# Efficient attention and RWKV channel mix on one core: a planner's order against a written order table, with another opening and another last store

## The chip, the core and the metric

The kernel runs on one core of one Trainium2 chip. The metric is the device time of one execution in microseconds (us). Engines: PE is the matrix engine (TensorE; PEld its weight loads), DVE VectorE, ACT ScalarE, POOL GpSimd, SP the engine that only issues transfers. PE, ACT, DVE and POOL each run their own instructions in the order in which the program lists them. Transfers issued on SP and ACT go to the hardware's queues, those issued on POOL to a software queue; the sixteen DMA engines serve all of them.

## The reference

```python
# q, k, v: (8, 8, 576, 64) = batch, heads, S, D
q_s = softmax of q over D; k_s = softmax of k over S
kv  = einsum('bhsd,bhse->bhde', k_s, v)
x   = einsum('bhsd,bhde->bhse', q_s, kv), heads joined: (8, 576, 512)
x_prev = x moved by one row (a row of zeros first)
xk = mu_k * x + (1 - mu_k) * x_prev
xr = mu_r * x + (1 - mu_r) * x_prev
k   = max(xk @ w_k, 0);  v = (k * k) @ w_v      # w_k 512 x 1024, w_v 1024 x 512
out = sigmoid(xr @ w_r) * v                       # w_r 512 x 512
```

## The kernel before

**Work.** Attention goes by items (b, g): batch b, and g = 0 or 1 for half of the heads. An item is named by its two digits, so `KV01` is the product of batch 0, half 1. The channel mix goes by units of 512 rows (256 in the last unit of each half of the batches), ten in all; unit 0 needs batch 0 alone.

**Steps of an item.** `load..q/k/v` (`load`, L248; halves `0` and `1` for batches 0 and 1), `expq` and `expk` (L383, ACT), `rsum`, `rrec`, `scale` (L398, L402, L407, DVE: the softmax of q), `T` (L417, PE: 18 transposes of the scaled q into PSUM), `KV` (L438, L441, PE: 72 products; those with a column of ones, L441, give the sum of exp(k) and lie in the PSUM bank in which `T` wrote), `qt` (L424 or L428, ACT: copies the transposed q out of that bank), `rz` and `kvn` (L451 or L455, L461, DVE: reciprocal of the sums, scaled kv). For batches 0 and 1 the mix with mu is folded into the weights: `wp` (L538, DVE, two multiplications for xk, m = 0, and two for xr, m = 1), `X` (L550, PE, 16 products, per m) and `x` (L560 or L563, one copy by ACT and one by DVE, to xk or xr). From batch 2 on, `X`, `T` and `KV` of two items make one PE block `B`, and the mix is done on DVE after it.

**Steps of a unit.** `k` (L687, PE, eight groups of four 128x512 matmuls, each followed by `relu` L672 on ACT and `sq` L676 on DVE), `r` (L719, PE; `th` L724 on ACT), `v` (L739, PE, two halves of four matmuls per tile of 128 rows), `o` (L745, DVE) and the store `st` (L757, two transfers for each tile). A last digit or `.2` tells halves: in unit 0, `k01.2` is the second half of group 1.

**mu.** `emit_mu` (L313) makes, on PE in f32 before anything else, a wide copy of mu (L315, `mu_wide`) and, with four pairs of small matmuls, its transpose (L318); ACT copies the first, DVE makes 1 - mu from it (L328, `emit_rest`).

**What sets the order.** `Plan.order` (L158) runs a list scheduler over all operations with an assumed duration for each, due times (`AHEAD`, `SOON`, `LOOK`) and the free buffers; the program is written in the order of its start times. `FIRST` sets the queues of batch 0: of its eight half loads of q and k, seven go on SP and one, of item 01, on ACT. `gate` holds w_k's first load, and with it all that follows on POOL, until the ACT load has landed (`weight`, L341). The tile framework adds the waits between instructions from the tiles that they touch, and gives every transfer on POOL one of eight semaphores, so that a transfer waits until the one eight places earlier has landed.

Of the kernel before, what the change touches and what calls it, by code (L numbers as in the profile page):

```python
# [8 lines left out]
ACT = mybir.ActivationFunctionType  # L9
# [24 lines left out]
START = 0.7  # L34
HOP = 0.05
LATE = 1e6
LOOK = {"PE": 0.03, "ACT": 0.2, "DVE": 0.1, "POOL": 0.03, "SP": 0.03}
MAIN = 5.676
PACE = 1.116
DMA_LEAD = 2.0  # L40
DMA_TAIL = 0.6
LOAD_RATE = 375.0
CAST_RATE = 375.0
GATE = 5
FUSED = (0, 1)
ROWS = 1.05
MU_EARLY = 3.0
BLOCK_LOOK = 0.4
EARLY_UNITS = 2
AHEAD = {(0, 0): 0, (0, 1): 0.64, (1, 0): 3.95, (1, 1): 5.45, (2, 0): 10.46, (2, 1): 5.14, (3,  # L50
        0): 9.42, (3, 1): 7.74, (4, 0): 0, (4, 1): 10.55, (5, 0): 2.05, (5, 1): 11.13, (6, 0):
        16.45, (6, 1): 16.13, (7, 0): 1.76, (7, 1): 3.64}
FIRST = ((0, 0, ("SP", "SP")), (0, 1, ("SP", "SP")), (1, 0, ("SP", "ACT")), (1, 1, ("SP",
        "SP")))
SOON = {(1, 0, 0): 4.53, (1, 0, 1): 4.87}
PASSES = 3


class Slot:

    def __init__(self, pool):
        self.pool = pool
        self.index = None
        self.rank = self.since = None
        self.last = []


class Op:

    def __init__(self, engine, occ, lat, key, emit, deps, takes, gives, size, rate, name):  # L70
        self.engine, self.occ, self.lat, self.key = engine, occ, lat, key
        self.emit, self.deps, self.takes = emit, list(deps), list(takes)
        self.size, self.rate, self.name = size, rate, name
        self.start = self.end = self.made = None
        self.early = 0.0
        self.main = False
        self.look = 0.0
        for slot in gives:
            slot.last.append(self)


class Plan:

    def __init__(self):
        self.pools = {name: [SHARED.get((name, i), [(name, i)]) for i in range(n)]
                      for name, n in POOLS.items()}
        self.ops = []

    def add(self, engine, occ, lat, key, emit, deps=(), takes=(), gives=(), size=0.0, rate=1.0,
            name=""):  # L90
        op = Op(engine, occ, lat, key, emit, [d for d in deps if d is not None], takes, gives,
                size, rate, name)
        self.ops.append(op)
        return op

    def places(self, op):
        t, got = 0.0, []
        for slot in op.takes:
            if slot.index is not None:
                t = max(t, slot.since)  # L100
                continue
            best = None
            if slot.rank is not None and slot.rank != self.next.get(slot.pool, 0):
                return None
            for i, parts in enumerate(self.pools[slot.pool]):
                if (slot.pool, i) in got:
                    continue
                free = 0.0
                for part in parts:
                    user = self.user.get(part)  # L110
                    if user is not None:
                        if not user.last or any(o.end is None for o in user.last):
                            free = None
                            break
                        free = max(free, max(o.end for o in user.last) + HOP)
                if free is not None and (best is None or free < best[0]):
                    best = (free, i)
            if best is None:
                return None
            t = max(t, best[0])  # L120
            got.append((slot.pool, best[1]))
        return t, got

    def warm(self, t):
        busy = 0.0
        for s, e in reversed(self.pe_busy):
            if e < t - 3.4:
                break
            busy += min(e, t) - max(s, t - 3.4)
        return busy > 2.0  # L130

    def set_due(self):
        for op in self.ops:
            op.due = op.key
        for op in reversed(self.sorted):
            if not op.size and not op.main:
                for o in self.after[op]:
                    op.due = min(op.due, o.due - op.lat - HOP)
                op.due -= op.early

    def prepare(self):
        self.after = {op: [] for op in self.ops}
        for op in self.ops:
            for d in op.deps:
                self.after[d].append(op)
        left = {op: len(op.deps) for op in self.ops}
        ready = [op for op in self.ops if not op.deps]
        self.sorted = []
        while ready:
            op = ready.pop()  # L150
            self.sorted.append(op)
            for o in self.after[op]:
                left[o] -= 1
                if not left[o]:
                    ready.append(o)
        assert len(self.sorted) == len(self.ops)

    def order(self):  # L158
        self.set_due()
        self.user = {}  # L160
        self.next = {}
        self.pe_busy = []
        dma_free = 0.0
        out = {"HW": [], "SW": []}
        free, able, done = {}, {}, []
        left = {}
        for op in self.ops:
            op.start = op.end = None
            for slot in op.takes:
                slot.index = None  # L170
            left[op] = len(op.deps)
            able.setdefault(op.engine, [])
            if not op.deps:
                able[op.engine].append(op)
        n = len(self.ops)
        while len(done) < n:
            chosen = None
            for engine, ops in able.items():
                now = free.get(engine, START)
                ready = None  # L180
                for op in ops:
                    t = now
                    for d in op.deps:
                        t = max(t, d.end + HOP)
                    if op.size:
                        ends = out["SW" if op.engine == "POOL" else "HW"]
                        if len(ends) >= 8:
                            t = max(t, ends[-8] + 0.3)
                    if op.takes:
                        found = self.places(op)  # L190
                        if found is None:
                            continue
                        t = max(t, found[0])
                    rank = (max(t - op.look, now + LOOK[engine]), op.due)
                    if ready is None or rank < ready[0]:
                        ready = (rank, t, op)
                if ready is not None and (chosen is None or ready[1] < chosen[1]):
                    chosen = ready
            assert chosen is not None, "no operation can start"
            _, t, op = chosen  # L200
            fresh = [slot for slot in op.takes if slot.index is None]
            for slot, (_, i) in zip(fresh, self.places(op)[1] if fresh else ()):
                slot.since = t
                slot.index = i
                if slot.rank is not None:
                    self.next[slot.pool] = slot.rank + 1
                for part in self.pools[slot.pool][slot.index]:
                    self.user[part] = slot
            occ, lat = op.occ, op.lat
            if op.engine == "PE" and not self.warm(t):  # L210
                occ, lat = 2 * occ, occ + lat
            op.start, op.end = t, t + lat
            if op.size and op.size < 20:
                op.end = t + lat + (2.0 if op.engine == "SP" else 8.0)
            elif op.size:
                dma_free = max(dma_free, t + DMA_LEAD) + op.size / op.rate
                op.end = dma_free + DMA_TAIL
            if op.size:
                out["SW" if op.engine == "POOL" else "HW"].append(op.end)
            if op.engine == "PE":  # L220
                self.pe_busy.append((t, t + occ))
            free[op.engine] = t + occ
            able[op.engine].remove(op)
            done.append(op)
            for o in self.after[op]:
                left[o] -= 1
                if not left[o]:
                    able.setdefault(o.engine, []).append(o)
        return sorted(done, key=lambda o: o.start)
# [681 lines left out]
```

## Time and profile before

| | |
|---|---|
| median of 3 runs | 205.75 us (205.47 to 206.05) |
| the profiled execution's own time | 205.87 us |
| its span, first to last instruction | 204.1 us |
| around the span (difference) | 1.8 us |
| PE busy | 187.9 us, 92% |
| DVE, ACT, POOL busy | 152.7, 146.8, 38.6 us |
| last matmul ends | 198.82 us |

How to read it: times in the views count from the first instruction of the span. A busy PE in the opening is not PE at full speed, since the length of a matmul's row there is about twice that of the same row later. POOL's busy time is mostly the issuing of transfers.

### The profile page before, as it was taken

The page shows a single profiled execution, that of the slowest core. Times are in us where ns is not written, and L with a number is a line of the kernel's source. Part 1 is how long each engine was busy: PE and PEld are TensorE (multiplying, and loading weights), DVE is VectorE, ACT ScalarE, POOL GpSimd, SP SyncE. Part 2 cuts the span into 40 slices and gives each one's busy share as a digit, 9 for nine tenths or more (in the row PEclk, how much of TensorE's full clock was granted, in tenths as well). Part 3 has the DMA queues.
Part 4 walks back from the last instruction along what each step waited for, and adds up shares of the span by engine and source line. Part 5 has one row for each costly group of instructions (what it writes and reads, how often), then busy time and mean ns, then how long its engine had stood idle before and what let it go on. Part 6 is the DMA issues. An engine that isn't in the chain of part 4 may idle for free.

```text
span 204.1 us, 4851 instructions
## 1 busy us (share of the span) xinstructions
PE 187.9 (92%) x1930; PEld 93.9 (46%) x1930; DVE 152.7 (75%) x348; ACT 146.8 (72%) x226; POOL 38.6 (19%) x61
## 2 busy tenths in 40 slices
PE   0659999979999999999999999999999999999990
PEld 0445444534454444444466444444444444444750
DVE  1865478999889989999999995999825459622620
ACT  4463689999999999999999488777624752642520
POOL 4912269433223312532000000000000000000000
PEclk9999999999999999999999999999999999999997
DMA  6999999999999994999742220422044012404303
GB/s 206 277 247 206 256 404 391 399 405 405 392 393 400 410 385 137 368 348 401 224 102 53 48 58 3 100 57 53 0 100 110 0 41 65 103 0 103 90 16 104
DMA packets 16431, 40.10 MB, mean 197 GB/s; under 512 B 2196, under 2 KB 5528, under 8 KB 16408
## 3 DMA queue, kind: packets, MB, share of 16 engines
q0 software_dynamic: 9328, 27.99, 41.6%
q1 hardware_dynamic: 6696, 11.25, 19.7%
q10 hardware_dynamic: 384, 0.56, 0.8%
q8 instruction: 15, 0.25, 0.5%
q14 instruction: 8, 0.07, 0.1%
HBM read 33.56 MB, written 9.44 MB: 211 GB/s over the span
## 4 chain that ended last, share of the span: by engine, by line
PE 78%; DMA 13%; DVE 3%; ACT 2%; POOL 1%; issue 0%; DVEq 0%; ACTq 0%
PE mm_b L739 9%; PE mm_c L739 9%; PE mm_d L739 7%; PE mm_b L687 7%; DMA wr<-in_moe_w_r_dram 7%; PE mm_c L687 7%; PE mm_d L687 7%; PE mm_a L687 7%; PE mm_a L719 6%; DMA raw_g<-in_v_dram 4%; PE mm_a L739 4%; PE mm_d L719 3%; PE mm_c L719 3%; PE mm_b L719 3%; DMA raw_b<-in_q_dram 2%; PE att_b L444 1%
## 5 line engine op out<-in xcount | busy, mean ns | idle before, releaser
L687 PEld LDWEIGHTS <-wk_a 128*128 128x128 bf16 x160 | 15.3, 99 | 17.0 <-issue 1.8
L687 PEld LDWEIGHTS <-wk_b 128*128 128x128 bf16 x160 | 15.5, 98 | 15.3 <-issue 0.2
L719 PEld LDWEIGHTS <-xr 128*128 128x128 bf16 x144 | 13.9, 98 | 16.8 <-ACT xr L563 0.9
L739 PEld LDWEIGHTS <-k_a 128*128 128x128 bf16 x144 | 13.8, 98 | 16.4
L739 PEld LDWEIGHTS <-k_b 128*128 128x128 bf16 x152 | 14.2, 98 | 14.7 <-issue 0.2
L719 PE MATMUL mm_a<-wr,xr 128*128 128x512 bf16 x56 | 14.4, 379 | 0.4 <-DMA raw_g<-in_v_dram 0.4
L724 ACT ACTIVATE th_a<-mm_a 128x512 f32<-128x512 f32 x14 | 8.4, 602 | 7.2 <-PE mm_a L719 7.1
L687 PE MATMUL mm_b<-xk,wk_a 128*128 128x512 bf16 (+1 forms) x44 | 11.2, 371 | 0.0
L687 PE MATMUL mm_c<-xk,wk_a 128*128 128x512 bf16 (+1 forms) x40 | 10.2, 371 | 0.0
L687 PE MATMUL mm_a<-xk,wk_a 128*128 128x512 bf16 (+1 forms) x40 | 9.8, 360 | 0.3 <-DVE xk L560 0.3
L687 PE MATMUL mm_c<-xk,wk_b 128*128 128x512 bf16 (+1 forms) x40 | 9.4, 358 | 0.0
L687 PE MATMUL mm_d<-xk,wk_b 128*128 128x512 bf16 (+1 forms) x40 | 9.4, 358 | 0.0
L687 PE MATMUL mm_a<-xk,wk_b 128*128 128x512 bf16 (+1 forms) x40 | 9.4, 358 | 0.0
L687 PE MATMUL mm_b<-xk,wk_b 128*128 128x512 bf16 (+1 forms) x40 | 9.4, 358 | 0.0
L687 PE MATMUL mm_d<-xk,wk_a 128*128 128x512 bf16 (+1 forms) x36 | 9.2, 368 | 0.0
L315 PE MATMUL mm_a<-mu_rows,pick 2*128 2x512 f32 x2 | 2.0, 1122 | 6.8 <-DMA mu_rows<-in_moe_mu_r_dram 6.8
L719 PE MATMUL mm_d<-wr,xr 128*128 128x512 bf16 x32 | 8.2, 379 | 0.0
L719 PE MATMUL mm_b<-wr,xr 128*128 128x512 bf16 x28 | 7.2, 379 | 0.0
L719 PE MATMUL mm_c<-wr,xr 128*128 128x512 bf16 x28 | 7.2, 379 | 0.0
L676 DVE TENSOR_TENSOR k_a<-rel_a 128x512 bf16<-128x512 bf16 (+1 forms) x13 | 5.1, 391 | 2.8 <-ACT rel_a L672 2.6
L672 ACT ACTIVATE rel_b<-mm_a 128x512 bf16<-128x512 f32 (+1 forms) x7 | 4.0, 571 | 4.1 <-PE mm_a L687 3.9
L676 DVE TENSOR_TENSOR k_a<-rel_c 128x512 bf16<-128x512 bf16 (+1 forms) x13 | 5.1, 392 | 2.4 <-ACT rel_c L672 2.3
(323 smaller groups left out, 487.7 us busy)
## 6 DMA issues: line engine op xcount, KB each, us to landing
out_dram<-ot_a SPq DMA_DIRECT2D x14, 128.0 KB, 2.4
out_dram<-ot_b SPq DMA_DIRECT2D x14, 128.0 KB, 2.4
out_dram<-ot_c SPq DMA_DIRECT2D x14, 128.0 KB, 3.2
out_dram<-ot_d SPq DMA_DIRECT2D x14, 128.0 KB, 2.7
raw_k<-in_v_dram POOLq DMA_DIRECT2D x3, 576.0 KB, 8.5
out_dram<-ot_e SPq DMA_DIRECT2D x13, 128.0 KB, 2.4
raw_j<-in_k_dram POOLq DMA_DIRECT2D x2, 576.0 KB, 10.7
raw_a<-in_q_dram POOLq DMA_DIRECT2D x2, 576.0 KB, 10.1
```

Source lines behind the costliest of these rows:

```text
L315: nc.tensor.matmul(kn.bank(wide_slot), lhsT=kn.pick[:].rearrange("p u c -> p (u c)"), rhs=kn.mu_rows[:].rearrange("p m c -> p (m c)"), sta ...
L444: kn.nc.tensor.matmul(to, lhsT=by, rhs=kn.vvs[vv.index][two[r], j, u, 0:65], **flags)
L672: kn.nc.scalar.activation(out=kn.rels[rel.index][:, 0:n], in_=kn.bank(kf)[:, 0:n], func=ACT.Relu, scale=HALF_ROOT)
L676: kn.nc.vector.tensor_tensor(out=kn.k2s[k2.index][:, fc, 0:n], in0=kn.rels[rel.index][:, 0:n], in1=kn.rels[rel.index][:, 0:n], op=ALU.mult)
L687: kn.nc.tensor.matmul(kn.bank(kf)[:, 0:n], lhsT=kn.wk[fc // 4][:, ct, (fc % 4) * 128:(fc % 4) * 128 + 128], rhs=kn.xs[0][:, ct, c0:c0 + n] ...
L719: kn.nc.tensor.matmul(kn.bank(rps), lhsT=kn.xs[1][:, ct, c:c + 128], rhs=kn.wr[:, ct, :], start=(ct == 0), stop=(ct == CT - 1))
L724: kn.nc.scalar.activation(out=kn.ths[th.index][:], in_=kn.bank(rps), func=ACT.Tanh, scale=0.5)
L739: kn.nc.tensor.matmul(kn.bank(vps)[:, 0:width], lhsT=kn.k2s[k2.index][:, ft, 128 * m:128 * m + 128], rhs=kn.wv[ft // 4][:, ft % 4, part], ...
```

## The change

The scheduler with its durations and due times is taken out. `ORDER` lists all operations in one sequence, with the buffers that each takes behind a colon and, for one load, the issuing engine ahead of an exclamation mark; each engine runs its own operations in that sequence. Besides the order itself:

- The gate on w_k's load is gone. Of batch 0's loads, the first half of q of item 00 goes on ACT, seven on SP. On POOL, `load00v` comes first, then half loads of batch 1 between `load01v`, `wk0` and, later, `wk1`, `wr`, `wv0`, `wv1`.
- Up to sixteen operations `fill` are defined, two matmuls of 256 columns on a tile of zeros (`still`); the table uses six (`fill`, `fill.2` to `fill.6`).
- `KV` of batch 0 is cut into `KV000`, `KV001` (one for each half load of k), each of 36 products.
- The wide copy of mu stays in the opening (`wide`, `widecopy`); 1 - mu is made on POOL (`rest`). The transposed mu is loaded by two POOL transfers (`muload`) and made by one transpose (`mu`, `mucopy`) in unit 1.
- `wp` for m = 1 moves from DVE to POOL.
- The two transfers of each store are operations of their own. In the last unit the second one of tile 0 goes on POOL; those of tile 1 are on SP and ACT.

```diff
-FIRST = ((0, 0, ("SP", "SP")), (0, 1, ("SP", "SP")), (1, 0, ("SP", "ACT")), (1, 1, ("SP",
-        "SP")))
-SOON = {(1, 0, 0): 4.53, (1, 0, 1): 4.87}
-PASSES = 3
+FILLS = 16
+FIRST = ((0, 0), (0, 1), (1, 0), (1, 1))
+
+ORDER = """
+ACT!load00q0:0 zero load00v load01q1:1 warm load01q0 load10k0:2 load00q1 load00k1:3 ident rows
+load01v load00k0 load10q1:4 load01k0:5 wk0 expq000:0 load11q1:6 load01k1 expq011:1 rsum000:0
+load10v0:7 expq010 load10q0 rsum010:1 expq001 consts rsum001 wide:0 rrec000 expk001:0 rrec010
+rrec001 scale000:0 scale001 fill:1 expk000 rsum011 T00:0 widecopy fill.2:2 scale010:1 KV000:1 rest
+fill.3:3 rrec011 expk010:1 scale011 fill.4:1 KV001 qt00:0 wk1 T01:3 rz00:0 kvn00:0 fill.5:0
+load10k1 expk011 KV010:1 edge00 late qt01:1 load11q0 KV011 wp000:0 fill.6:1 rz01:1 expq101:2
+X000:0.2 kvn01:1 edge01 wp010:1 wp011 x0000 x0001 X010:3.1 wr k01:1 x0100 x0101 load11v0:8 k02:0
+expq111:0 rsum101:2 k03:2 load11k0:9 k00:3 load10v1 X011:0.1 expq100 k03.2 muload x0111 cast100:0
+k02.2 rsum100 k00.2 expk100:2 k01.2 wp001 x0110 relu02:0 load11v1 sq02:0 k04:0 rrec100 rsum111:3
+expk101 load11k1 X001:1.0 relu01:1 wv0 relu03:2 k06:1 expq110 sq03 rrec101 x0010 sq01 k05:2 x0011
+relu00:0 rsum110 relu04:2 r02:3 relu05:1 wv1 scale100:2 cast110:1 r01:0 sq05 load20v0:10 rrec111
...
+sq95 st82.2 v910:0 v811 r90:1 o81:4 k97:2 st81 th90:1 v900:3 relu97:0 sq97 v910.2:1 v911
+v911.2 v901 o90:2 o91.2:3 st90.2 st90 o91 st91.4 st91 st91.2 st91.3
+"""
...
+    def ordered(self):
+        ops = {op.name: op for op in self.ops}
...
+        for token in ORDER.split():
+            name, _, places = token.partition(":")
+            name, _, held = name.partition("^")
+            engine, _, name = name.rpartition("!")
+            op = ops[name]
+            if engine:
+                op.engine = engine
...
+            yield op
...
-    gate = [first[GATE]]
-        if gated:
-            kn.tc.add_manual_dep(ld.ins, gate[0].made.ins.name, sync)
...
-        for i in range(4):
-            nc.tensor.matmul(
-                kn.bank(mu_slot)[:, 2 * i:2 * i + 2],
-                lhsT=kn.mu_rows[:].rearrange("p m c -> p (m c)")[:, 128 * i:128 * i + 128],
-                rhs=kn.pick[:, :, 0], start=True, stop=True)
+    def emit_mu():
+        kn.nc.tensor.transpose(out=kn.bank(mu_slot)[:, 0:8], in_=kn.mu_sb[:],
+                               identity=kn.identf[:])
...
+        kn.nc.gpsimd.tensor_scalar(out=kn.mu_wide[:, 1, :], in0=kn.mu_wide[:, 0, :],
+                                   scalar1=-1.0, scalar2=1.0, op0=ALU.mult, op1=ALU.add)
...
+        def fill(slot=slot):
+            for _ in range(2):
+                kn.nc.tensor.matmul(kn.bank(slot)[:, 0:256], lhsT=kn.ident[:],
+                                    rhs=kn.still[:], start=True, stop=True)
...
-            kvm = add("PE", 0.9, 1.0, step, lambda: kv(kvp), before_kv + [tr], [kvp], leave_kv,
-                      name=f"KV{tag}")
+            kvm = tr
+            for u in range(2):
+                kvm = add("PE", lambda u=u: kv(kvp, (u,)), [expk[u], castv[0], consts, kvm], [kvp], leave_kv if u else [], name=f"KV{tag}{u}")
...
-                    kn.nc.vector.tensor_tensor(
+                    (kn.nc.gpsimd if m else kn.nc.vector).tensor_tensor(
...
-                        q = kn.nc.scalar if len(parts) == 2 and i == 1 else kn.nc.sync
+                    if last and m >= tiles - 2:
+                        queue = ("SP", "ACT" if len(parts) == 2 else "POOL")[i]
```

In the table's last line `o90` is the 512-column gate of tile 0 of the last unit (its matmuls `v901` are the last of the program); `o91` and `o91.2` are the two 256-column halves of tile 1, whose matmuls `v911` and `v911.2` come just ahead of `v901`. Before, DVE's order at the end is tile 0, then tile 1's first half, then its second half, whose matmuls come last.

## The prediction

> **What bounds the kernel now.** I read the page first, then busy time by stretch, then the timeline of PE in the opening, the waits, and the timeline of the last six microseconds.
>
> ```profile
> PE 187.9 (92%) x1930; PEld 93.9 (46%) x1930; DVE 152.7 (75%) x348; ACT 146.8 (72%) x226; POOL 38.6 (19%) x61
> ...
> 10.00:17.57 7.57, 5.40 (x199) 4.63 (x199) 5.15 (x15) 5.27 (x10) 1.08 (x2) 1.00 1.21 238
> 17.57:21.16 3.59, 3.59 (x26) 1.27 (x22) 1.42 (x7) 0.18 (x1) 0.72 (x2) 1.00 1.22 203
> 21.16:30.00 8.84, 8.11 (x67) 3.73 (x64) 5.61 (x13) 6.82 (x14) 3.69 (x8) 1.00 1.12 336
> 40.00:60.00 20.00, 18.85 (x245) 8.99 (x244) 18.75 (x38) 19.97 (x28) 6.85 (x10) 1.00 1.03 399
> 60.00:190.00 130.00, 130.00 (x1188) 62.09 (x1187) 103.61 (x225) 96.17 (x144) 11.97 (x17) 1.00 0.47 148
> ```
>
> In the stretches (length, then busy PE, PEld, DVE, ACT, POOL) PE is busy for all of 60 to 190 us. So the end is the moment at which unit 0's first `k` starts (17.57), plus a fixed amount of PE work, plus PE's idle and half-speed time behind that moment, plus the tail. Idle time behind it is small: 0.34 us at 22.11 and 1.15 us near 43. Half-speed time shows in the rows:
>
> ```profile
> 17.57 1.03 PE L687 MATMUL mm_a<-xk,wk_a 128*128 128x512 bf16 x2
> 18.39 1.06 PE L687 MATMUL mm_b<-xk,wk_a 128*128 128x512 bf16 x2
> 21.16 0.61 PE L687 MATMUL mm_d<-xk,wk_a 128*128 128x512 bf16 x2
> 22.55 0.59 PE L687 MATMUL mm_b<-xk,wk_a 128*128 128x512 bf16 x2
> 22.98 0.59 PE L687 MATMUL mm_c<-xk,wk_a 128*128 128x512 bf16 x2
> ```
>
> Two matmuls take 0.82 us from start to start at 17.57 and 0.43 at 22.55; the granted-clock column reads 1.00 in both stretches, so it does not show this. From 17.57 to 21.16 PE did three such pairs (1.29 at full speed) and one `X` (0.6 with the change of tile shape) in 3.59 us: 1.7 us lost to half speed.
>
> **The opening, as changed.** "Two hardware queues" is not new: one half load was on ACT before too. From issue time and time to landing, the SP half loads of before landed, in the queue's order, at 4.4, 5.3, 6.1, 8.6, 10.3, 11.7, 13.2. POOL's queue runs beside them from about 5 us in both kernels, so the same places give about the same times. In the new order they hold q of 01, q of 01, q of 00, k of 00 (no longer behind mu: 7.7), mu, k of 00 (10.1), k of 01 (11.7), k of 01 (13.3). Ungating w_k puts more behind v on POOL but takes no more of a shared rate; its first transfer starts 0.7 us earlier. I charge nothing; if POOL takes a larger share the chain shifts by up to 0.7.
>
> Now PE's order. mu lands 0.7 behind the load ahead of it (6.11 to 6.82 before), so at 8.4. `wide` takes 1.84 (6.82 to 8.66): 10.2. `fill`, two matmuls of half the width of the 17.57 row, 0.43: 10.7. `T00` 0.6 (10.29 to 10.88): 11.3. `fill.2`: 11.7. `KV000`, half of 13.32 to 14.40: 12.3. `fill.3`, `fill.4`: 13.1. `KV001`: 13.7, result 13.9. The three waits that follow come from one order: `qt00` now stands behind `KV001`, which writes the same PSUM bank. Before it stood ahead, and the sums waited for it:
>
> ```profile
> PE att_a L441 <- ACT qt_a L424: 1.0, 1, 1.0
> PE att_b L438 <- ACT ek_a L383: 0.9, 1, 0.9
> PE att_a L550 <- ACT xk L560: 1.2, 1, 1.2
> ```
>
> `qt00` (1.12) ends at 15.1; queued behind it on ACT is the second exp of k of 01, though its data lies ready (13.3): 15.7. `rz00` and `kvn00` (0.16 and 0.29) end at 15.6; `KV010` overwrites the bank that `kvn00` read, so 15.6 to 16.2. `qt01`, two copies (0.53 and 0.64), to 17.5; `KV011` writes its sums into the banks just read, so 17.5 to 18.2 with its result. `rz01` 0.25, `kvn01` 0.29, `wp010` 0.49: 19.2. Meanwhile `fill.6` and `X000` (0.94 at half speed, 15.37 to 16.32) go from 18.1 to 19.5; `X010` follows to 20.4; copies of `X000` (0.64 on ACT, two of 0.45 on DVE) end by 20.3. So `k01` starts near 20.4, 2.8 later than before. In that time `X010` is done too, worth 0.6: net 2.2 behind.
>
> What comes back. Before, the first full-speed row came 3.3 to 3.6 us behind the first dense one (17.57). Now dense work starts with `fill.6` at 18.1, so full speed at about 21.6, 1.2 us into `k`: 0.6 lost where 1.7 was, gain 1.1. The second gain is the idle time. `X011` (before, X waited for copies, and 0.34 and 1.15 were lost) now has other groups of `k` around it, and batch 1's attention is drawn forward to the first unit. If nothing new waits, 1.5 us come back. PE's end: 198.82 + 2.2 - 1.1 - 1.5 = 198.4.
>
> **Work moved to POOL.** DVE loses 0.69 (`rest`) and eight `wp` of 0.285. No row shows these on POOL; its affine select on 128x128 takes 0.29, its longest issue 0.84. I take 0.45 for a `wp`, with those two as bounds. `wp011` starts at 19.0 and `X011` is due at 22.1 behind four half groups: covered up to 1.5 each. Behind `wp011` on POOL stands `wr`'s issue (20), then five half loads of batch 1, two mu transfers, `wp001`, `wv0`, `wv1`. The queue's earlier bytes run out near 21.5, so `wr` (2.6 us, the spacing of w_k, w_r, w_v landings before) lands at 25 to 26, while `r02` is due at 27.5; `wv0` lands near 32, `v010` is due near 33.5. Cover of 1.5 us, not more. `muload`'s second transfer waits for `wk1` (about 21), and `wp001` behind it is due at 25. The Trainium skill, "GPSIMD Engine Reference", section "4.1 Engine selection", speaks against this move: it gives two-input elementwise work on GpSimd as about twice as slow as on VectorE. By that an estimate is 0.57 for a `wp`; the sum would stay. The transposed mu leaves the opening (1.63 us, 8.66 to 10.29) and costs one small matmul and its load in unit 1, under 0.1 on PE; that gain is inside the chain above, where the fills take 1.7 of it back. `identf` and the memset of `still` add about 0.2 to DVE ahead of 7.7, where `T00` is not due before 10.7: nothing. `KV` in two halves issues the same 72 products; its price is the order above. Single stores and the new column of mu in `scale_x` cost nothing that a row shows.
>
> **The tail.**
>
> ```profile
> 198.22 0.60 PE L739 MATMUL mm_a<-wv_b,k_b 128*128 128x256 bf16 x4
> 198.86 0.42 DVE L745 SCALAR_TENSOR_TENSOR ot_a<-th_b,mm_a 128x256 f32<-128x256 f32 x1 [0.24 <-PE mm_a L739]
> 198.88 1.19 SPq L757 DMA_DIRECT2D out_dram<-ot_a  x2
> 198.97 1.58 ACTq L757 DMA_DIRECT2D out_dram<-ot_a  x2
> ```
>
> Before, one gate of 0.42 follows the last matmul, and the span ends 5.28 behind it. Now `v901` is last and DVE runs `o90`, `o91.2`, `o91` behind it: starts 0.61 and 0.34 apart, the last ends 1.40 behind PE instead of 0.46. `o91.2` and `o91` had their matmuls 0.9 and 1.3 earlier, but stand behind `o90`. The two pairs of stores follow as before, so 0.94 later: 6.2 behind PE. `o90`'s POOL store starts at 0.8; with `vb_a`'s first-transfer delay as the upper bound (7.5 to landing with its data, 3.9 to its first packet) it could end last by up to a microsecond; the other loads on POOL bound it at 4, hidden. I take hidden.
>
> **Sum.** 198.4 + 6.2 = 204.6 of span, and 1.8 around it: 206.4, against 205.87 of the profiled execution (the median is 205.75). About 0.6 us (0.3%) is what a measurement of this kernel can tell.
>
> **The rivals.**
> *The zeros do their work (faster).* PE is busy from 8.4 on, and if full speed comes by about 12, `fill.3` to `X010` shrink by 0.9 and nothing is lost in `k` (0.6): 204.9. For it: six fills are dense. Against it: before, PE was busy for 5 of the 7.5 us from 10 to 17.57 and stayed at half speed. It decides if the first `k` row reads 0.43 per pair and starts before 19.5.
> *Full speed comes a window later (slower).* If dense work from 18.1 misses the moment, `k` runs at half speed for 4 to 5 us: 1.4 to 1.9 more lost, 208.1. The Trainium skill, "TensorE: Matmul & The Clock Gate", section "What's actually happening", says that the clock is judged over free-running windows of about 3.4 us, so a start inside one waits for the next. The 3.3 us of before agree with one whole window; the trace cannot show where it began.
> *A wait takes the place of the removed ones (slower).* `r02`, `v010` or `X011` wait on POOL's queue, or the 1.5 us of idle time reappear: 207.5 to 208.
> *The table does nothing that PE can feel* (dense part and opening cancel, tail overlapped): 205.5 to 206.2.
>
> **How the numbers follow.** Forecast, 206.0 to 206.9, 0.42, a third of it inside the bound. Zeros effective, 204.4 to 205.3, 0.23. Later window, 0.13. New wait or late POOL store, 0.12. Cancelling, 0.10. Faster: 0.23 and a little of the last: 0.25. Slower: 0.28 + 0.13 + 0.12 = 0.53. Same: 0.22. The range takes in the rivals on both sides, without the outer half of those that end late.
>
> **What would show it.** Right: `wide` near 8.4, `qt00` near 14, `k01` near 20.4, PE end near 198.4, DVE's last gate 1.4 behind it. Wrong: `k01` before 19, PE idle again between 22 and 45, a POOL row of `wp` over 1.5 us, or an end less than 5.6 behind PE.

## The result, and the profile after

The changed kernel takes 212.33 us (median of 4 runs, 211.38 to 212.61) against 205.68 for the kernel of before on the same chip: a ratio of 1.031, 95% interval 1.028 to 1.035. It is slower, as forecast, but by 6.7 us where 0.7 were forecast, and outside the range: the slowest rival on record stood at 208.1. The profiled execution of the changed kernel took 212.61, of it 210.8 of span.

From the page, the engines' busy time; then busy time by stretch (length, then busy PE, PEld, DVE, ACT, POOL; granted clock, DMA share, GB/s) for the opening, the first 6 us of `k`, and the two stretches behind:

```profile
PE 191.3 (91%) x1935; PEld 94.6 (45%) x1935; DVE 150.7 (71%) x341; ACT 146.6 (70%) x225; POOL 44.4 (21%) x73
```
```profile
10.00:24.21 14.21, 12.58 (x227) 7.68 (x226) 5.62 (x24) 6.54 (x11) 4.32 (x8) 1.00 0.94 251
24.21:30.00 5.79, 5.79 (x36) 2.38 (x36) 3.59 (x7) 4.52 (x9) 4.69 (x10) 1.00 0.92 219
30.00:60.00 30.00, 29.86 (x409) 14.34 (x408) 25.91 (x55) 28.49 (x44) 16.76 (x25) 1.00 1.02 329
60.00:190.00 130.00, 129.20 (x1190) 62.33 (x1189) 106.40 (x232) 98.79 (x149) 12.28 (x17) 1.00 0.50 164
```

The first `k` starts at 24.21 (17.57 before), although PE is busy for 12.6 of the 14.2 us ahead of it: the opening is for the most part not waiting, it is working. Behind it PE is idle for 0.14 near 41 and 0.80 between 60 and 190, where before it was never idle in the latter. The opening on PE's timeline:

```profile
9.65 2.04 PE L252 MATMUL mm_a<-mu_rows,pick 2*128 2x512 f32 x2 [9.65 <-DMA mu_rows<-in_moe_mu_r_dram]
11.62 0.61 PE L284 MATMUL mm_b<-still,ident 128*128 128x256 bf16 x2
12.16 0.66 PE L358 MATMUL att_a<-ident,qs_a 64*128 64x64 bf16 x18
...
13.29 0.27 PE L379 MATMUL att_b<-vb_a,ek_a 64*64 64x64 bf16 x2
...
14.22 0.20 PE L382 MATMUL att_a<-one,ek_a 64*64 64x1 bf16 x2
14.35 0.61 PE L284 MATMUL mm_d<-still,ident 128*128 128x256 bf16 x2
14.75 0.63 PE L284 MATMUL mm_b<-still,ident 128*128 128x256 bf16 x2
15.31 0.27 PE L379 MATMUL att_b<-vb_a,ek_a 64*64 64x64 bf16 x2
...
24.21 1.01 PE L589 MATMUL mm_b<-xk,wk_a 128*128 128x512 bf16 x2
25.02 1.06 PE L589 MATMUL mm_a<-xk,wk_a 128*128 128x512 bf16 x2
```

`wide` is 1.25 later than forecast. One half of the first sums step, 36 products, runs from 13.29 to 14.35: 1.06 us, as long as 68 of the 72 products took before (13.32 to 14.40; the other four had run earlier). The `k` pairs still start 0.8 apart: half speed. Further back, a late store on the chain of waits, and the rows of PE and VectorE where PE's 0.80 of idle time arises:

```profile
64.29 8.09 DMA out_dram<-ot_b
```
```profile
72.03 1.02 PE L589 MATMUL mm_a<-xk,wk_a 128*128 128x512 bf16 x4 [0.64 <-DVE ot_e L646]
73.21 1.02 PE L589 MATMUL mm_c<-xk,wk_b 128*128 128x512 bf16 x4 [0.16 <-DVE ot_b L646]
```

```profile
71.29 0.69 DVE L646 SCALAR_TENSOR_TENSOR ot_e<-th_a,mm_a 128x512 f32<-128x512 f32 x1 [1.34 <-DMA out_dram<-ot_e]
72.47 0.69 DVE L646 SCALAR_TENSOR_TENSOR ot_b<-th_b,mm_c 128x512 f32<-128x512 f32 x1 [0.49 <-DMA out_dram<-ot_b]
```

These are two waits, not one. The larger, 0.64, is the gate `o13` (71.29): the table gives it the buffer `ot_e`, which `o11` had used (62.42). That tile's two stores were issued right behind their gate, at 63.13 and 63.65, and the second landed at 71.17 in the trace's records, 7.5 us after its issue. The smaller, 0.16, is `o12` (72.47), which takes `ot_b`. The other half of that tile was stored at 44.54; this half, `st00.2`, stands behind `st03` and `st11` in SP's order, is issued 20 us later and lands at 72.38. The end:

```profile
202.53 1.03 PE L640 MATMUL mm_d<-wv_b,k_b 128*128 128x512 bf16 x4
203.59 0.69 DVE L646 SCALAR_TENSOR_TENSOR ot_c<-th_b,mm_d 128x512 f32<-128x512 f32 x1 [2.28 <-PE mm_d L640]
...
204.53 0.41 DVE L646 SCALAR_TENSOR_TENSOR ot_d<-th_a,mm_a 128x256 f32<-128x256 f32 x1
204.58 0.57 POOL L656 DMA_DIRECT2D out_dram<-ot_c  x1 [98.62 <-DVE ot_c L646]
...
204.97 1.14 SPq L656 DMA_DIRECT2D out_dram<-ot_d  x2
```

The last gate ends 1.38 behind PE (203.56), as forecast, and the last store lands at 208.32. But the span ends at 210.83, 2.5 behind that landing, where before it was 1.2 (202.86, 204.07). In the trace's records SP's closing drain ends at 208.77, and POOL's, which begins with its store at 204.55, ends at 210.05, though that store landed at 207.63.

### The profile page after: what moved, and what is told of

Its sections match the earlier page's. It is cut to its first block, busy times and chain, and to the rows that moved or that the text cites. A ratio compares the mean times of both kernels' runs of the same rounds, so it can differ in the third digit from the quotient of the medians.

```text
span 210.8 us, 4855 instructions
## 1 busy us (share of the span) xinstructions
PE 191.3 (91%) x1935; PEld 94.6 (45%) x1935; DVE 150.7 (71%) x341; ACT 146.6 (70%) x225; POOL 44.4 (21%) x73
## 4 chain that ended last, share of the span: by engine, by line
issue 48%; PE 31%; DMA 7%; DVE 6%; ACT 2%; SPq 1%; POOL 1%; POOLq 0%; DVEq 0%
PE mm_c L589 4%; DMA out_dram<-ot_b 4%; PE mm_a L589 3%; DMA mu_rows<-in_moe_mu_r_dram 3%; PE mm_d L589 3%; PE mm_b L589 3%; PE mm_a L640 2%; PE att_b L379 2%; PE mm_d L620 1%; PE mm_b L640 1%; PE mm_d L640 1%; PE att_a L473 1%; PE att_b L473 1%; PE mm_a L252 1%; PE mm_b L620 1%
## 5 line engine op out<-in xcount | busy, mean ns | idle before, releaser
L589 PE MATMUL mm_b<-xk,wk_b 128*128 128x512 bf16 (+1 forms) x56 | 13.1, 357 | 0.0
L589 PE MATMUL mm_d<-xk,wk_a 128*128 128x512 bf16 (+1 forms) x48 | 11.8, 361 | 0.0
L620 PE MATMUL mm_d<-wr,xr 128*128 128x512 bf16 x44 | 11.3, 380 | 0.0
L589 PE MATMUL mm_a<-xk,wk_a 128*128 128x512 bf16 (+1 forms) x40 | 10.6, 381 | 0.6 <-DVE ot_e L646 0.6
L620 PE MATMUL mm_b<-wr,xr 128*128 128x512 bf16 x40 | 10.3, 379 | 0.0
L589 PE MATMUL mm_d<-xk,wk_b 128*128 128x512 bf16 x36 | 9.2, 379 | 0.0
L589 PE MATMUL mm_b<-xk,wk_a 128*128 128x512 bf16 (+1 forms) x32 | 7.7, 354 | 0.1
L640 PE MATMUL mm_a<-wv_a,k_a 128*128 128x512 bf16 x28 | 7.2, 380 | 0.0
L640 PE MATMUL mm_a<-wv_b,k_a 128*128 128x512 bf16 x28 | 7.2, 379 | 0.0
L620 PE MATMUL mm_a<-wr,xr 128*128 128x512 bf16 x28 | 7.2, 379 | 0.0
L589 PE MATMUL mm_c<-xk,wk_b 128*128 128x512 bf16 (+1 forms) x32 | 6.9, 339 | 0.2 <-DVE ot_b L646 0.2
```

The source lines that it names most:

```text
L589: kn.nc.tensor.matmul(kn.bank(kf)[:, 0:n], lhsT=kn.wk[fc // 4][:, ct, (fc % 4) * 128:(fc % 4) * 128 + 128], rhs=kn.xs[0][:, ct, c0:c0 + n] ...
L620: kn.nc.tensor.matmul(kn.bank(rps), lhsT=kn.xs[1][:, ct, c:c + 128], rhs=kn.wr[:, ct, :], start=(ct == 0), stop=(ct == CT - 1))
L640: kn.nc.tensor.matmul(kn.bank(vps)[:, 0:width], lhsT=kn.k2s[k2.index][:, ft, 128 * m:128 * m + 128], rhs=kn.wv[ft // 4][:, ft % 4, part], ...
```

## The experiments

The theory after this reading: four separate costs, namely the sums in two steps, the fills, the late half store (to which it put down all of the 0.80), and the store on POOL, beside loads that land later. The rivals, for each, stand in the expectations. Times are medians, with the ratio to before from the same chip; "T00 to k" is the time from `T00`'s start to the first `k`, which leaves most of the effect of the loads out (12.05 in the changed kernel).

**e1, sums in one step.**
```
-            for u in range(2):
-                kvm = add("PE", lambda u=u: kv(kvp, (u,)), [expk[u], ...
+            kvm = add("PE", lambda: kv(kvp), expk + [castv[0], consts, kvm], ...
```


> The changed kernel with each b0 sums step (72 products) in one piece again, at the place of the second half. Theory A (a half of 36 products takes PE as long as the whole did, 1.06 us, so the two-step form costs 2.1 us on the opening chain): the second piece still takes 1.06 and the first is gone; unit 0's first k goes from 24.21 to about 22.1, and the time from 212.3 to about 210.2. Rival (a half costs half, and the late opening is the loads alone): the merged piece takes 2.1, first k stays within 0.3 of 24.2 and the time within 0.4 of 212.3.


209.54, 1.019 (1.015 to 1.023). T00 to k 9.58: 2.5 less; the loads were 0.9 earlier as well. PE's timeline of e1:

```profile
12.72 0.63 PE L282 MATMUL mm_b<-still,ident 128*128 128x256 bf16 x2
13.29 0.28 PE L377 MATMUL att_b<-vb_a,ek_a 64*64 64x64 bf16 x4
...
14.13 0.18 PE L380 MATMUL att_a<-one,ek_a 64*64 64x1 bf16 x4
...
14.61 0.39 PE L282 MATMUL mm_a<-still,ident 128*128 128x256 bf16 x2
...
18.16 0.61 PE L282 MATMUL mm_b<-still,ident 128*128 128x256 bf16 x2
...
38.01 1.02 PE L637 MATMUL mm_a<-wv_b,k_a 128*128 128x512 bf16 x4 [0.83 <-DMA wv_b<-in_moe_w_v_dram]
```

Four products stand in a row where the halves had two, and the last of all 72 starts 0.84 behind the first, the last rows already at full speed (see the last section). Theory A holds in kind. The 2.5 has a little of that full speed in it; e2 and e8 below, two kernels without fills that show none in the opening, are 1.7 apart with and without halves (e8 has edits to stores and POOL's queue besides). The last row of the view: with the opening shorter, `w_v` is too late, the wait that the prediction had named as a rival and that the late opening had hidden.

**e2, no fills** (the `fill` tokens taken out of the table).


> The changed kernel without its six groups of zero matmuls. Theory A (the zeros stand on the chain and bring no clock): the opening loses fill.2, fill.3, fill.4 from its chain (0.55 + 1.0), first k near 22.7, the same 0.8 us lost to half speed in k: 210.8. Rival (the zeros bring the clock forward): first k near 22.7, but half speed lasts 1.5 us longer into k, so the time stays at 212.3 within 0.4.


210.70, 1.025 (1.019 to 1.031). T00 to k 10.02, 2.0 less. Full speed came 2.5 to 4.0 us into `k` (1.9 in the changed kernel). Theory A by the time and for the chain. The profiled execution took 212.18, the slowest of four (209.39 to 212.18), and in it half speed lasts 2.0 longer into `k`, as the rival has it. Kernels that keep the fills show full speed anywhere from 0.4 to 3.8 behind the first `k` too, so this one profile does not decide for the rival.

**e3, stores at their gates.** In the table `st00.2` and the others follow their gates, and `o13:4 ... o12:1` becomes `o13:1 ... o12:4`.


> The changed kernel with SP's stores in the order of their gates, the two halves of a tile side by side (and output buffers 1 and 4 exchanged for o13 and o12, so that the one with the earlier store is used first). Theory A (PE's 0.8 us of idle time at 71 to 73 comes from one late half store, issued 20 us after its gate): no idle PE row between 60 and 200, PE's end 0.8 to 1.0 earlier, 211.4. Rival (the stores land late because the loads hold the DMA engines, wherever they are issued): 0.5 us or more of idle time stays at 70 to 75, and the time is within 0.4 of 212.3.


212.18, 1.031 (1.027 to 1.034). The 0.80 of idle time became 0.25, 0.4 more was lost to half speed in `k`, and PE's end came 0.5 earlier in the profile; in the times there is no difference: inconclusive alone. The edit has two parts. The exchange of the buffers bears on the 0.64: `o13` now takes a buffer that is free (70.30 instead of 71.29). The stores of `o11` still take 7.4 and 7.9 us to land, as the rival says, and `o12`, which now takes their buffer, is the 0.25 that is left. e8, with the same edit, has no such idle time; e1, e2, e4, e7, e13 and e14, without it, have 0.7 to 0.9 before the same gate.

**e4, the late store off POOL.**
```
-                        queue = ("SP", "ACT" if len(parts) == 2 else "POOL")[i]
+                        queue = ("SP", "ACT")[i]
```


> The changed kernel with the one late store that GpSimd issues (half of the tile o90) issued by ScalarE instead. Theory A (GpSimd's closing drain ends 2.4 us behind its own store's landing and 1.3 behind SP's drain, and so sets the end): the span ends 6.0 behind PE instead of 7.2, time 211.1. Rival (the three gates and pairs of stores behind the last matmul set the end, GpSimd's drain is covered): the end stays 7.0 or more behind PE, time within 0.3 of 212.3.


210.56, 1.024 (1.019 to 1.029). The end is 5.70 behind PE instead of 7.27. Theory A. (PE's end was 0.5 earlier as well, with full speed 0.4 behind the first `k`; the edit touches nothing there.)

**e5, the kernel of before with its sums in two passes.**
```
-            for j in range(J):
-                for u in range(2):
+            for u, j in ([(u, j) for u in range(2) for j in range(J)] if b == 0 else
+                         [(u, j) for j in range(J) for u in range(2)]):
```


> The kernel of before with one edit: in each of batch 0's two sums steps, all 36 products of the first half stand ahead of all 36 of the second, instead of alternating. Same instructions, same places for the step as a whole. Theory A (products of the two halves run beside each other on PE only when they alternate): each step takes 2.1 us instead of 1.08, first k from 17.57 to about 19.6, time 207.8. Rival (a product costs what it costs, 0.015 us, in any order): steps of 1.08, 205.7 within 0.3.


207.06, 1.0055 (1.003 to 1.008). The second step:

```profile
17.07 0.26 PE L439 MATMUL att_b<-vb_b,ek_b 64*64 64x64 bf16 x2
...
18.87 0.19 PE L442 MATMUL mm_d<-one,ek_b 64*64 64x1 bf16 x1
19.00 0.61 PE L688 MATMUL mm_a<-xk,wk_a 128*128 128x512 bf16 x1
```

From its first to its last start it takes 1.80, against 1.13 before (16.32 to 17.45), from nothing but the order of the same products. T00 to k is 7.96 instead of 7.28. Theory A in kind, 0.7 where it expected 2.0: the first step costs nothing, since its first half runs in the 0.89 that PE had waited for `k`'s exp. The other half of the 1.4 in time would be the loads, which were 0.75 later in this profile; why they were is not shown.

**e6, the kernel of before with two late stores on POOL** (`kn.nc.gpsimd` where `part.stop == C`). The expectation speaks of one; the edit also moves the second half of the last unit's next-to-last tile, whose part ends at C as well (198.90).


> The kernel of before with one edit: of the last tile's four half stores, the one that ScalarE issues last is issued by GpSimd. Theory A (a store on GpSimd's queue at the end holds GpSimd's closing drain 5.5 us from its issue, as in the changed kernel, 204.58 to 210.05): drain ends near 205.0, span near 205.7 instead of 204.1, time 207.3. Rival (GpSimd's store is as good as ScalarE's, and the longer tail of the changed kernel comes from three gates): 205.7 within 0.4.


207.62, 1.009 (1.006 to 1.013). From the timeline and from the chain:

```profile
199.88 0.55 POOL L757 DMA_DIRECT2D out_dram<-ot_a  x1 [0.43 <-DVE ot_a L745]
```
```profile
199.86 0.57 POOLq L906
```

POOL's drain runs from 199.86 to 205.16, 2.0 behind SP's (203.12). Theory A, shown a second time, though not for one store alone.

**e7, mu ahead of the first half load of k** (the token `rows` moved).


> The changed kernel with the mu rows loaded ahead of the first k half load, where before had them, instead of behind it. Theory A (the fifth half load falls into the pause of 5.5 to 7 us that GpSimd's first packets cause in SP's queue, and mu stands behind it): wide starts near 7.3 instead of 9.6, T00 near 10.2 instead of 12.2, first k 1.3 to 1.7 earlier, time 210.8. Rival (the chain runs through k's loads, which the mu rows push back): first k within 0.4 of 24.2, time within 0.4 of 212.3.


211.48, 1.029 (1.025 to 1.032). `wide` 7.59, `T00` 10.14, first `k` 22.24; T00 to k 12.10, unchanged. Theory A for the opening, 2.0 earlier; but 1.17 of idle time appeared at 93, again a gate that waits for a store (the buffer's store lands at 93.05, the gate starts at 93.13), and of the 2.0 only 0.85 is left.

**e8, the four together,** with `wr` ahead of `wp011` and `muload` behind `load20q0` on POOL.


> The changed kernel with the edits of e1, e2, e3 and e4 together, and on GpSimd's queue w_r ahead of the opening's wp, and the late mu transfers behind batch 2's first loads. Theory A (the four causes are separate and add up): first k near 18.7, no idle time over 0.3 behind it, full speed within 1.5 us of it, PE's end near 198, the end 5.7 behind it: span 203.7, time 205.4, even with before. Rival (w_v's loads are late once the opening is faster, as the 0.83 us wait at 37 in e1 shows): 1 to 2 us of idle time between 33 and 45, time 207.


205.35, 0.998 (0.996 to 1.0005). First `k` 19.55, idle time 0.14, PE's end 197.83, the end 5.69 behind it. Theory A: the costs add up (2.8, 1.6, 0.2 and 1.8 alone make 6.4, together 7.0), though the first `k` comes 0.85 later than it expected.

**e9 to e12, from e8 on.** e9: `v901 v910.2 ... v911 v911.2`, the gates and stores in that order. e10: `load10k0` behind `wk0`. e11: `nc.vector` for all `wp`. e12: `X000:0.2 KV011:1 ... k01:1 k02:0 X010:0.1`.


> e8 with PE's last products in another order: the full-width v901 ahead of the four half-width ones, so that a gate of 0.42 is last, as before. Theory A (one gate behind PE instead of three, as in before): the end 5.0 to 5.3 behind PE instead of 5.7, time 204.8. Rival (the landing of the stores, 3.4 behind the last gate, is set by how many are open at once, and they still come together): the end stays 5.6 or more behind PE, 205.3.


204.08, 0.992 (0.989 to 0.995). The end is 4.37 behind PE: Theory A, and more.


> e9 with the one half load of batch 1 that stands second on GpSimd's queue (2.3 KB packets, between the two v of batch 0) moved behind w_k's first half. Theory A (its packets take the DMA engines from SP's loads, which landed up to 1.2 later than before's): SP's last four half loads land 0.4 to 0.7 earlier, first k 0.4 earlier, time 204.4. Rival (SP's loads share packet by packet with whatever GpSimd sends): landings within 0.2, time within 0.3 of e9.


203.93, 0.991 (0.988 to 0.994), the same as e9. Three of SP's last half loads land 0.4 earlier than in e9 (8.8, 10.6 and 12.5), and the first `k` comes 0.4 earlier, as Theory A has it; but e11 and e12, with e9's loads, have 10.6 and 12.2 too. Not told apart.


> e9 with the four wp of m = 1 on VectorE again (the first of them behind the copies of X010). Theory A (wp010 on VectorE takes 0.75 instead of 0.45 because GpSimd's wp runs beside it, and this stands on the chain): the wp010 row 0.45, first k 0.3 earlier, time 204.5. Rival (VectorE needs the time that GpSimd took off it): first k as in e9, and 0.3 to 0.6 of idle PE time between 22 and 45, time 205.1.


202.91, 0.987 (0.984 to 0.990). `wp010` takes 0.49 (0.75 in e9), but T00 to k is 8.21 against 8.25: what it saves is hidden. PE's end is 1.13 earlier than in e9: 0.6 by the loads (`T00`), 0.13 of idle time, 0.1 of half speed; the rest was not found in rows.


> e9 with X000 ahead of the second sums step and X010 behind the first two groups of k, as before had it. Theory A (what counts is the total of PE's opening work and its half-speed time, not when k starts): first k near 17.8 instead of 19.5, but two more k groups at half speed and X010 to do; PE's end within 0.3 of e9, time 204.8. Rival (an earlier k is worth its whole lead): PE's end 1.0 or more earlier, time 203.6.


203.45, 0.990 (0.987 to 0.994). First `k` at 17.13, 2.7 earlier; PE's end 0.9 earlier: by these numbers and the time nearer to the rival. But `T00`, which the edit does not touch, is 0.6 earlier, and the 0.3 that is left is what Theory A has. Not told apart.

**e13 to e15.** e13: the changed kernel with `nc.vector` for all `wp`. e14: `memset(kn.still[:], 1.0)`. e15: e11 with e12's order.


> The changed kernel with one edit: the four wp of m = 1 on VectorE again, the first of them behind the copies of X010. Theory A (the move to GpSimd, priced at nothing, costs by itself: the loads of w_r and w_v and the copies behind wp on VectorE come later): first k 0.2 to 0.3 earlier, time 211.3 or less. Rival (the move is covered in the changed kernel, whose late opening leaves room): time within 0.4 of 212.3.


210.72, 1.025 (1.022 to 1.029). Faster by 1.6, as Theory A wants, but not by its mechanism: T00 to k is 12.04, `T00` itself 0.9 earlier (nothing ahead of it was touched), and full speed came 0.4 behind the first `k` instead of 1.9. What the move of `wp` costs by itself stays open; on the chain from `T00` to `k` it is nothing.


> The changed kernel with one edit: the fills multiply ones where they multiplied zeros. Theory A (it is not the zeros: the fills are too few and too spread to bring the clock, whatever they hold): the fills stay at 0.186 from one matmul to the next, full speed again only from 24.5 to 27, time within 0.4 of 212.3. Rival (zeros do not count as work for the clock, ones do): full speed before 17, the second sums step and X at half their time, first k near 21.5, time 209.


213.07, 1.034 (1.030 to 1.038). Fills 0.186 apart, full speed at 25.2: Theory A by these signs. The time is 0.7 over that of the changed kernel, outside the 0.4 that it allowed, with overlapping intervals; its profile has 1.27 of idle time at 95 before a gate, where the changed kernel, the same but for one constant, has none.


> e11 with the order of e12 in the opening (X000 ahead of the second sums step, X010 behind two groups of k). Theory A (PE's total counts, not the start of k): within 0.4 of e11, 202.7. Rival (the gains of e11 and e12 add up): 202.2 or less.


202.95, 0.987 (0.984 to 0.989): Theory A by the time. In the profile `T00` is 0.65 later than in e11 and PE's end 0.16 earlier, so what this order is worth stays open. e9 to e12 and e15 are all faster than the kernel of before, e11 and e15 by 1.3%. Of e11, the two stretches that had idle time in the changed kernel:

```profile
30.00:60.00 30.00, 30.00 (x454) 14.69 (x453) 26.45 (x58) 28.73 (x42) 12.98 (x18) 1.00 1.06 381
60.00:190.00 130.00, 130.00 (x1144) 63.02 (x1142) 103.04 (x225) 95.00 (x145) 10.84 (x15) 1.00 0.47 147
```

## Why the prediction was wrong in size

The direction held, and so did the frame: the first `k`, plus PE's work, plus what is lost, plus the tail. But the 0.7 of the forecast was hardly more than the 0.6 that it called measurable, the small rest of terms that cancelled, and most of the 6.7 comes from terms that it had too small or at nothing: that the sign came out right says little for the sum. By its terms, against the profiled execution:

| term | forecast | measured | more |
|---|---|---|---|
| `wide` starts | 8.4 | 9.65 | 1.25 |
| from there to the first `k` | 12.0 | 14.56 | 2.56 |
| lost to half speed in `k` | 0.6 | 0.9 | 0.3 |
| idle behind the first `k` | 0 | 0.94 | 0.94 |
| the end behind PE | 6.2 | 7.27 | 1.07 |
| time | 206.4 | 212.6 | 6.2 |

**The step that failed most: "`KV000`, half of 13.32 to 14.40", and "`KV` in two halves issues the same 72 products; its price is the order above".** A half takes as long as the whole. In the rows of before, four products share each 0.05 us, two for each half of the output partitions; in the changed kernel two do. The forecast counted products; it should have looked at which of them ran side by side. Four halves at 0.95 to 1.06 where 0.6 to 0.7 was taken are 1.5 of the 2.56; e1 (2.5 on T00 to k, with some full speed in it), e8 against e2 (1.7) and e5 (0.7 on one step) show it. Of the rest, 0.5 is the fills and 0.3 `X010` (22.98 to 24.21, where 0.9 was taken). The Trainium skill, "TensorEngine Tiling (Array Packing)", section "Key Properties", says that different tiles of the array work independently and in parallel; the traces agree: 1.1 us with the halves alternating, 1.8 with one behind the other.

**"mu lands 0.7 behind the load ahead of it, so at 8.4."** The gap of before between 6.11 and 8.62 was put down to mu. It is a pause in SP's queue itself: the load in that place landed at 9.17 with no mu ahead of it, and e7 puts mu before the pause: it lands at 7.02 there (9.52 in the changed kernel), and `wide`, which then waits for `pick` on VectorE, starts at 7.59. `qt00`, forecast near 14, started at 16.49.

**"If nothing new waits, 1.5 us come back."** The old idle time did go. It was 1.9, not 1.5: in the stretch from 21.16 to 30.00 the prediction counted 0.34 where 8.84 less 8.11 is 0.73 (a wait of 0.40 ends at 28.98). What was not followed is which buffer each gate takes and when that buffer's store lands: `o13` with the buffer of `o11` (0.64), `st00.2` behind `st11` (0.16). The prediction costed single stores at "nothing that a row shows"; the rival of a new wait was looked for on POOL's queue, where none came in the changed kernel (`wp` 0.44 to 0.51 each, forecast 0.45).

**"I take hidden"**, of POOL's store. The bound of a microsecond was not wide enough: e4 takes 1.57 off the end, e6, with two stores, puts 1.67 on it (6.92 behind PE instead of 5.25).

**What was right.** The fills cost on the chain, though more than the 1.7 of the forecast: `wide` to the first `k` is 14.56 with them and 12.00 in e2. In the changed kernel they brought no clock (e14: ones neither). Three gates behind PE: 1.38 for 1.4; e9 takes that back. `wp` on POOL is covered on the chain (e11, e13: 0.0).

**Open.** Kernels with the same opening loads have `wide` anywhere from 8.77 to 9.65, and full speed from 0.4 to 4.0 behind the first `k`. Differences below 1 us between two kernels (e10, e11, e12, e14, e15, part of e13) can't be put down to an edit by one profile, even where their times are apart.

## What to carry to other kernels

Before a group of small matmuls is split, see in the rows how many start in the same instant: splitting along the axis that runs in parallel halves nothing. Follow each queue's order to its last instruction, stores too, and ask of each gate which buffer it takes and when that buffer's last store lands. Keep transfers on GpSimd away from a kernel's last microseconds.

## What the runs showed of the hardware

**GpSimd's closing drain** ended 5.5 us behind the issue of its last store in the changed kernel (204.58, 210.05) and 5.3 in e6 (199.88, 205.16), 2.4 behind the landing in the former. It is 5.45 to 5.51 in all seven kernels that issue one such store there (the changed one, e1, e2, e3, e7, e13, e14). No row tells what it waits for.

**The clock came and went in one window.** In e1 the first rows at full speed are near 14.0 (the fill at 14.61 takes 0.39 where others take 0.61 to 0.64), the last near 17.4, and full speed is back with the first `k` at 20.88: 3.4 us on, at most 3.5 off. The Trainium skill, "TensorE: Matmul & The Clock Gate", section "What's actually happening", gives free-running windows of about 3.4 us; this agrees. The changed kernel was busy without a break from 9.65 to 17.57, longer than two such windows, and stayed at half speed, with the same fills; in e1 the sums ran four products at a time. e8 to e12 and e15 run them so without fills, and show no full speed in the opening either. So it came in the one kernel that has both; that the two together are the reason was not tried, and it is one profile.
